# Value products and transposes share two PSUM banks, the MoE output product is turned, and one softmax addition goes to GpSimd

## The chip, the cores and the metric

The kernel runs on one core of one Trainium2 chip. The metric is the device time of one launch in microseconds, as the median of several runs. The profile is that of one more execution, taken by the hardware profiler.

## The reference, cut to what matters

Three stages follow each other: attention that keeps the 32 largest scores of each query, a gated MLP ("MoE 1") and a second MLP with a cosine ("MoE 2"). All arrays are float32.

```python
# q, k, v: (4, 8, 576, 64), batch x heads x sequence x head size
scores = (q @ k.transpose(0, 1, 3, 2)) / sqrt(64)
kth = np.partition(scores, -32, axis=-1)[..., -32:-31]
scores = np.where(scores >= kth, scores, -1e9)
attn = np.exp(scores - scores.max(-1, keepdims=True))
attn = attn / (attn.sum(-1, keepdims=True) + 1e-9)
x = (attn @ v).transpose(0, 2, 1, 3).reshape(2304, 512)

g = x @ w_gate                      # 512 x 1536
x = (g / (1 + exp(-g)) * (x @ w_val)) @ w_out      # 1536 x 512

h = x @ w_in                        # 512 x 2048
out = (h * cos(h)) @ w_out2         # 2048 x 512
```

## The kernel before, in words

**Chunks and units.** The 2304 tokens are cut into ten chunks (`SIZES`, 18 tiles of 128 tokens): two of one tile, "turned" and computed in plain float32, and eight of two tiles, where each operand is split into a high and a low part in a faster float type and each product is three matmuls (high by high, low by high, high by low). A chunk has four head pairs p, and a unit is one tile of one head: 144 units. For a unit, TensorE makes the scores in the two banks `sc` (L572 or L579), ScalarE copies them out (`s`, L584), and VectorE finds the 32 largest by four MAX8 (L609) with three MATCH_REPLACE8 (L612) between. GpSimd makes two bounds of 128x2 and 128x1 (`b`, L623, L627), and ScalarE masks and exponentiates with them (`e`, L640, L651) and sums the row into `sm`.

**From the exponentials to x.** When both heads of a tile are done, TensorE turns `e` in three groups of four, four and one 128x128 transposes into one PSUM bank `tp` (L673), each fetched by ScalarE into `pt` (L679). `tp` is one buffer: a group waits until the one before is fetched (`r_tp = Ring(1)`). When all tiles of a chunk and head pair are in `pt`, `av_proc` multiplies by V into a bank of its own, `av` (L716, L719). Beside it `x_proc` adds 1e-9 to the sums and takes the reciprocal on VectorE, spreads it on GpSimd, turns it in a `tp` buffer, copies it out, and waits for `av` only then:

```python
        yield ("DVE", 0.2, lambda: nc.vector.tensor_scalar(smT[c, p], smT[c, p], 1e-9, None, op0=OP.add), due,
               True)
        yield "DVE", 0.09, rinv, due, True
```

This happens 40 times (ten chunks by four head pairs). ScalarE then copies `av` out (L771), GpSimd multiplies, and the product is split into `XH` and `XL`, which lie in two buffers of a whole chunk each.

**MoE 1.** Per chunk there are twelve steps f. `gemm_proc` makes gate and value for 128 of the 1536 columns (24 matmuls of 256 columns, `gv`, for the last chunk `gvl`, L868). ScalarE and GpSimd make the gated product and split it into `gh` and `gl` (two buffers, `r_g = Ring(2)`), and `wout_proc` (L1146) adds the step to the output product: with the weights `wo` as the held operand and the tokens moving, for each of four 128-column pieces d and three terms one matmul of 256 columns, twelve per step, into two banks `yt`, which hold the transposed result of the chunk:

```python
            def part(d, f=f, k=k):
                w = WO[k]
                gh, gl = G[c, f]
                for i, (a, m) in enumerate(((0, gh), (0, gl), (1, gh))):
                    nc.tensor.matmul(y1p[d // 2][:, d % 2], w[:, a, d * 128:d * 128 + 128], m, ...)
```

After the twelfth step four ScalarE copies through one tile `yo` (L1167), each followed by a store to `y1` in DRAM, free both banks for the next chunk (`r_y1p = Ring(1)`). A copy waits until the store of the one before has landed. For the last chunk but one (`late`) the four copies go to four tiles of their own and wait for no store. The two turned chunks have the tokens held and the weights moving, and turn their result back through `tp` (L1083 to L1123).

**MoE 2.** Six blocks of 384 tokens by sixteen steps: `h` (L1342, 12 matmuls of 384 columns), the cosine on ScalarE and VectorE, and `o` (L1407, 9 matmuls of 512 columns). Its weights `w2` take the place of those of MoE 1 as the steps of the last chunk end (L1270, L1274).

**What sets the order.** Nothing is scheduled at run time. A planner (`class Plan`) runs generators as processes: each step names an engine, a cost, a function that issues the instructions, and a due time. Whenever an engine comes free in the plan, the ready step with the smallest due time is issued, so that each engine gets one fixed queue. `Ring` gives the buffers, `Event` the dependences. On the chip each queue runs in that order and waits on semaphores. All loads and stores named here are issued by SyncE, in its own fixed order. Due times follow `PACE = 4.97` us per unit, and MoE 1 of a chunk is due during the attention of the next.

Of the kernel before, what the change touches and what calls it, by code (L numbers as in the profile page):

```python
# [23 lines left out]
NTOK = B * S  # L24
# [6 lines left out]
CH = 256  # L31
SIZES = (1, 1) + (2,) * 8
# [4 lines left out]
NP = H // 2  # L37
CB = 384
# [120 lines left out]
def topk_attention_moe_moe(ctx: ExitStack, tc: tile.TileContext, qT, kT, vP, w1, wo1, w2, out):  # L159
# [32 lines left out]
    yt = [psL.tile([128, DM], F32, tag=f"y{i}", name=f"y{i}") for i in range(2)]  # L192
    y1p = [x.rearrange("p (a b) -> p a b", a=2) for x in yt]
    sc = psR.tile([128, 2, 512], F32, name="sc")
    av = psR.tile([128, CH], F32, name="av")
# [9 lines left out]
    unit_of = {x: u for u, x in enumerate(units)}  # L205
    NU = len(units)
# [5 lines left out]
    def due_unit(u):  # L212
# [8 lines left out]
            xp.tile([128, 2 * DM], I32, tag="xl", name="c1", bufs=2)[:, :DM]]  # L221
# [46 lines left out]
    def w1_rest(i, raw, due):  # L268
# [4 lines left out]
        r_pre.free(i, t, plan)  # L273
        ev_w1x[f].set(t, plan)
# [110 lines left out]
    kfirst, klast, vfirst = {}, {}, {}  # L385
    for u, (c, p, t, h) in enumerate(units):
        for b, r0, r1 in segments(FIRST[c] + t):
            kfirst.setdefault((c, p, h, b), u)
            klast[c, p, h, b] = u
            vfirst.setdefault((c, p, b), u)  # L390
    vvis = {key: i for i, key in enumerate(vfirst)}
# [12 lines left out]
    ev_q = {(c, p, h): Event() for c in range(NCH) for p in range(NP) for h in range(2)}  # L404
# [10 lines left out]
    def q_due(c, p):  # L415
        return due_unit(unit_of[c, p, 0, 0]) - 25.0

    split = sorted([(k_due(b, p, h), 0, b, p, h) for b, p, h in kb_first] +
                   [(q_due(c, p), 1, c, p) for c in range(RAWC, NCH) for p in range(NP)])
# [5 lines left out]
    def q_index(c, p, h=0):  # L425
        return c * NP + p if c < RAWC else RAWC * NP + ((c - RAWC) * NP + p) * 2 + h

# [37 lines left out]
    def k_proc(i, b, p, h):  # L465
        due = k_due(b, p, h)
        n = NP + kvis[b, p, h]
# [21 lines left out]
    def q_proc(k, c, p):  # L489
        n = SIZES[c] * 128  # L490
        due = q_due(c, p)
# [3 lines left out]
        def load():  # L495
            st["x"] = att.tile([128, 2, HALF], F32, tag="raw", name="qx", bufs=r_kp.n)[:, :, :n]
            for s in range(2):
                nc.sync.dma_start(st["x"][64 * s:64 * s + 64], qT[p, :, FIRST[c] * 128:FIRST[c] * 128 + n]
                                  .rearrange("(h d) n -> d h n", h=2))

        yield "DMA", 1.1, load, due - 10.0, True
        for h in range(2):
            yield r_q.gate(q_index(c, p, h))

            def hi(h=h):
                Q[c, p, h] = att.tile([128, 2, CH], F32R, tag="q", name="q", bufs=r_q.n)[:, :, :n]
                nc.scalar.activation(Q[c, p, h][:, 0], st["x"][:, h], AF.Copy)
# [3 lines left out]
                       lambda h=h: nc.gpsimd.tensor_sub(Q[c, p, h][:, 1], st["x"][:, h], Q[c, p, h][:, 0]),  # L511
                       due + 2.0 * h, True)
            ev_q[c, p, h].set(t, plan)
# [20 lines left out]
    r_s, r_sc, r_w, r_e, r_pt, r_tp, r_av = Ring(5), Ring(1), Ring(2), Ring(2), Ring(1), Ring(1), Ring(1)  # L534
# [3 lines left out]
    eT, smT, ptT, XH, XL = {}, {}, {}, {}, {}  # L538
    ev_x = [Event(NP) for _ in range(NCH)]
    ev_av = {(c, p): Event() for c in range(NCH) for p in range(NP)}  # L540
    ev_pt = {(c, p): Event(SIZES[c]) for c in range(NCH) for p in range(NP)}
    ev_sum = {(c, p): Event(2 * SIZES[c]) for c in range(NCH) for p in range(NP)}
    r_x, r_rs = Ring(2), Ring(1)
    XW = (PLAIN + 1) // 2
    for i in range(XW):
        r_x.freed[i] = Event(min(2, PLAIN - 2 * i))
    xw = {}

    def x_index(c):
        return c // 2 if c < PLAIN else c - PLAIN + XW  # L550

    tp_count = [0]

    def unit_proc(u):
# [3 lines left out]
        st = {}  # L558
        if c < RAWC:
            yield ev_kr[p]  # L560
            yield ev_qr[c, p]
        else:
            for b, r0, r1 in segs:
                yield ev_k[b, p, h]
            yield ev_q[c, p, h]
            q = Q[c, p, h]
        yield r_s.gate(u)

        def qk():
# [5 lines left out]
            for b, r0, r1 in segs[::-1]:  # L575
                k = K[b, p, h]
                for s in range(2):
                    for a in range(2):
                        nc.tensor.matmul(sc[:r1, s, :HALF], q[:, a, t * 128:t * 128 + r1],  # L579
# [8 lines left out]
        if h and (c, t) == (RAWC - 1, SIZES[c] - 1):  # L588
            r_k.free(p, end, plan)
        for b, r0, r1 in segs:  # L590
            if c >= RAWC and kb_last[b, p, h] == u:
                r_k.free(NP + kvis[b, p, h], end, plan)
        if t == SIZES[c] - 1 and (h or c >= RAWC):
            r_q.free(q_index(c, p, h), end, plan)
# [52 lines left out]
        def expo():  # L647
            if (c, p) not in smT:
                smT[c, p] = att.tile([128, 4], F32, tag="sm", name="sm", bufs=3)[:, :2 * SIZES[c]]
            j = 2 * t + h  # L650
            nc.scalar.activation(st["e"], st["e"], AF.Exp, bias=st["b"][:, 2:3], scale=1.0,  # L651
                                 accum_out=smT[c, p][:, j:j + 1])
# [3 lines left out]
        ev_sum[c, p].set(end, plan)  # L656
# [3 lines left out]
    def group_proc(c, p, t, g, made, done):  # L660
# [17 lines left out]
        def fetch():  # L678
            nc.scalar.activation(ptT[c, p][:, j0:j1, t * 128:t * 128 + 128], st["ps"][:, :j1 - j0], AF.Copy)  # L679
# [5 lines left out]
    def pair_proc(c, p, t):  # L685
# [3 lines left out]
        yield r_pt.gate(c * NP + p)  # L689

        def alloc():
            if (c, p) not in ptT:
                ptT[c, p] = att.tile([128, 9, CH], F32, tag="pt", name="pt", bufs=r_pt.n)[:, :, :SIZES[c] * 128]

        now = yield "-", 0.0, alloc, 0.0, True
        made, done = Event(3), Event(3)
        for g in range(3):
            plan.start(group_proc(c, p, t, g, made, done), now)
# [3 lines left out]
        ev_pt[c, p].set(done.time, plan)  # L702

    def av_proc(c, p):
        n = SIZES[c]
        yield ev_pt[c, p]
        segs = segments(FIRST[c], n)
        for b, r0, r1 in segs:
            yield ev_v[c, p, b]
        yield r_av.gate(c * NP + p)  # L710

        def attv():
            pt = ptT.pop((c, p))
# [800 lines left out]
```

## Time and profile before

| | us |
|---|---|
| median of three runs | 1269.52 (1268.78 to 1275.1) |
| the profiled execution, its own time | 1267.64 |
| its span, first to last instruction | 1265.9 |
| attention's last MAX8 ends | some 771 |
| last x of attention | 793.5 |
| MoE 2 alone on TensorE | 868.4 to 1262.3 |

The span is what the trace covers. The time of the profiled execution is 1.7 us longer, and the median of the runs 1.9 us longer again. Times are microseconds from the span's start. TensorE's busy time takes in the pipelined tails of its matmuls, so that the length of a run of matmuls is read from the chain of waits, where their starts are told.

### The profile page before, as it was taken

Reading aid. Unit: us, or ns where it says so; the run is one execution under the profiler, and the core shown is the slowest. Engines: PE = TensorE matmul, PEld = TensorE weight load, DVE = VectorE, ACT = ScalarE, POOL = GpSimd, SP = SyncE. Lnnn points to the kernel's source line nnn. Section 1 sums busy time; section 2 is a strip of 40 time slices with the busy share of each in tenths; the row PEclk is TensorE's granted clock in tenths of the full one; section 3 lists DMA queues with packets and bytes.
Section 4 is the critical chain, followed back from the end, with each engine's and each line's share of the span. In section 5 each row is a group of like instructions: output and inputs, shape, how many; then the busy total and the mean of one; then the engine's idle time right before and its main releaser. Section 6 shows DMA issues by size and latency. Waiting matters only on the chain. (4 is left out here: it accounts for less than half of the span.)

```text
span 1265.9 us, 23359 instructions
## 1 busy us (share of the span) xinstructions
PE 1206.7 (95%) x8040; PEld 1075.1 (85%) x8040; DVE 989.1 (78%) x1978; ACT 916.8 (72%) x2049; POOL 622.8 (49%) x1042
## 2 busy tenths in 40 slices
PE   6699978999999999999999999998999999999998
PEld 3486646998998999889989989997999898999997
DVE  7999999999999999989999993347555555555554
ACT  4689998988998898888887876446555655565554
POOL 4797975776787776777675655543010101010000
PEclk9799989999999999999999999998999999999999
DMA  7645536666566655556553332781010101010000
GB/s 251 200 132 185 172 108 193 206 202 205 170 194 186 192 187 179 179 171 213 188 171 118 114 115 84 250 274 38 1 50 1 51 1 51 1 38 1 12 14 26
DMA packets 84455, 162.20 MB, mean 128 GB/s; under 512 B 17008, under 2 KB 40048, under 8 KB 84336
## 3 DMA queue, kind: packets, MB, share of 16 engines
q1 hardware_dynamic: 84176, 160.65, 39.6%
q8 instruction: 63, 1.03, 0.3%
q14 instruction: 56, 0.46, 0.1%
q10 hardware_dynamic: 160, 0.07, 0.0%
HBM read 133.41 MB, written 27.26 MB: 127 GB/s over the span
## 5 line engine op out<-in xcount | busy, mean ns | idle before, releaser
L609 DVE MAX8 m<-w 128x8 f32<-128x576 f32 x432 | 310.6, 747 | 2.0
L868 PE MATMUL gv<-xh,w 128*128 128x256 f32 x1344 | 289.4, 292 | 2.6 <-ACT hg L836 2.5
L868 PEld LDWEIGHTS gv<-xh,w 128*128 128x128 f32 x1344 | 225.9, 190 | 9.8 <-issue 4.8
L1342 PE MATMUL h<-x2h,w 128*128 128x384 f32 x768 | 214.4, 339 | 1.9 <-DVE g L1376 1.9
L612 DVE MATCH_REPLACE8 w<-m,w 128x576 f32<-128x576 f32 x288 | 212.5, 741 | 0.0
L1407 PE MATMUL o<-w,gh 128*128 128x512 f32 x576 | 196.1, 395 | 0.0
L868 PE MATMUL gv<-xl,w 128*128 128x256 f32 x672 | 189.5, 282 | 0.0
L1146 PE MATMUL y<-gh,wo 128*128 128x256 f32 x768 | 156.8, 287 | 6.3 <-DMA wo<-wo 5.2
L1305 POOL TENSOR_TENSOR x2l<-x,x2h 128x384 fp32r<-128x384 f32 x24 | 25.9, 1078 | 265.7 <-ACT x2h L1294 260.5
L1376 DVE TENSOR_TENSOR g<-r,h 128x384 f32<-128x384 f32 x96 | 53.2, 554 | 121.6 <-ACT r L1371 121.6
L1342 PEld LDWEIGHTS h<-x2h,w 128*128 128x128 f32 x768 | 141.4, 189 | 6.4 <-DVE g L1376 2.3
L1146 PEld LDWEIGHTS y<-gh,wo 128*128 128x128 f32 x768 | 126.5, 192 | 10.6 <-issue 5.9
L1342 PE MATMUL h<-x2l,w 128*128 128x384 f32 x384 | 129.8, 338 | 0.0
L868 PEld LDWEIGHTS gv<-xl,w 128*128 128x128 f32 x672 | 127.9, 190 | 0.2 <-issue 0.2
L673 PE MATMUL tp<-ident,e 128*128 128x128 f32 x648 | 110.7, 281 | 17.5 <-ACT pt L679 15.7
L1369 ACT ACTIVATE r<-r 128x384 f32<-128x384 f32 x96 | 50.3, 524 | 105.3 <-DVE r L1366 105.2
L1407 PEld LDWEIGHTS o<-w,gh 128*128 128x128 f32 x576 | 108.5, 188 | 21.2
L679 ACT ACTIVATE pt<-tp 128x512 f32<-128x512 f32 (+1 forms) x216 | 107.1, 496 | 24.7 <-PE tp L673 23.7
L609 DVE MAX8 m<-s 128x8 f32<-128x576 f32 x144 | 106.0, 744 | 14.5 <-ACT s L584 14.3
L640 ACT ACTIVATE e<-s,b 128x576 f32<-128x576 f32 x144 | 112.7, 783 | 5.1 <-POOL b L623 5.0
L651 ACT ACTIVATE e<-e,b 128x576 f32<-128x576 f32 x144 | 113.1, 785 | 1.9 <-POOL b L627 0.3
L1146 PE MATMUL y<-gl,wo 128*128 128x256 f32 x384 | 111.0, 289 | 2.9 <-DVE gl L930 1.5
(112 smaller groups left out, 2768.8 us busy)
## 6 DMA issues: line engine op xcount, KB each, us to landing
wo<-wo SPq DMA_DIRECT2D x96, 512.0 KB, 3.6
w_raw<-in_w SPq DMA_DIRECT2D x32, 511.8 KB, 4.3
V<-in_vP SPq DMA_DIRECT2D x52, 256.0 KB, 3.0
w<-in_w SPq DMA_DIRECT2D x24, 511.5 KB, 5.5
kx<-in_kT SPq DMA_DIRECT2D x64, 144.0 KB, 3.0
wo<-wo SPq DMA_DIRECT2D x36, 256.0 KB, 3.1
w2d<-w_raw SPq DMA_DIRECT2D x32, 256.0 KB, 2.5
cvx<-w2d SPq DMA_DIRECT2D x32, 256.0 KB, 4.6
```

Source lines behind the costliest of these rows:

```text
L609: nc.vector.max(out=st["m"][:, 8 * i:8 * i + 8], in_=st["w"] if i else st["s"])
L612: nc.vector.match_replace(out=st["w"], in_to_replace=st["m"][:, 8 * i:8 * i + 8], in_values=st["w"] if i else st["s"], imm_value=LOWEST)
L640: nc.scalar.activation(st["e"], st["s"], AF.Prelu, bias=st["b"][:, 1:2], scale=SCALE, alpha=STEEP)
L651: nc.scalar.activation(st["e"], st["e"], AF.Exp, bias=st["b"][:, 2:3], scale=1.0, accum_out=smT[c, p][:, j:j + 1])
L673: nc.tensor.transpose(st["ps"][:, j - j0], e[:, j * 128:j * 128 + 128], ident)
L679: nc.scalar.activation(ptT[c, p][:, j0:j1, t * 128:t * 128 + 128], st["ps"][:, :j1 - j0], AF.Copy)
L868: nc.tensor.matmul(gv[g], W1[f, kk // 2][:, a, g, kk % 2], m[:, kk], start=kk == 0 and i == 0, stop=kk == KT - 1 and i == 2)
L1146: nc.tensor.matmul(y1p[d // 2][:, d % 2], w[:, a, d * 128:d * 128 + 128], m, start=f == 0 and i == 0 and d % 2 == 0, stop=f == NF1 - 1 and ...
L1342: nc.tensor.matmul(st["h"], w[:, a, kk * 128:kk * 128 + 128], m[:, kk], start=kk == 0 and n == 0, stop=kk == KT - 1 and n == 2)
L1369: yield "ACT", 0.41, lambda: nc.scalar.activation(r, r, AF.Abs), due, True
L1376: nc.vector.tensor_mul(st["g"], r, h)
L1407: nc.tensor.matmul(o[t], a[:, cs], W2[f, 1][:, m], start=f == 0 and n == 0, stop=f == NF2 - 1 and n == 2)
```

## The change

- The bank `av` is gone. `tp` has two buffers, and the value product takes one of them; before it does so it waits for the copy of the spread reciprocal (`ev_rs`), because its own copy goes into that reciprocal's tile.
- The addition of 1e-9 goes from VectorE to GpSimd; the reciprocal stays on VectorE.
- In the output product of all chunks the tokens are held and the weights move: for each of the two tiles and three terms one matmul of 512 columns, six per step. The result has tokens on the partitions, so each tile is turned back: per half of a bank a ScalarE copy to `yo`, two transposes into the same half, a second ScalarE copy, and a store. Each bank now has its own ring, one tile each.
- The four tiles of their own for the last chunk but one go; all copies use the one `yo` tile.
- `XH`/`XL` are eight slots, one for each chunk and head pair, freed one by one after the last matmul that reads them. A scratch tile of the weight conversion goes from a slot of x to one of the ten `K` buffers.
- `ATT` would allow attention groups of two tiles and one tile; with the sizes at hand every chunk has one group, as before. Code for a turned last chunk goes; it was not reached.

```diff
-    r_s, r_sc, r_w, r_e, r_pt, r_tp, r_av = Ring(5), Ring(1), Ring(2), Ring(2), Ring(1), Ring(1), Ring(1)
+    r_s, r_sc, r_w, r_e, r_pt, r_tp = Ring(5), Ring(1), Ring(2), Ring(2), Ring(1), Ring(2)
...
+        yield ev_rs[key]
+        k = tp_count[0]
+        tp_count[0] += 1
+        yield r_tp.gate(k)
...
+            av = st["av"] = psR.tile([128, 4, 128], F32, tag="tp", name="av", bufs=r_tp.n).rearrange(
+                "p a b -> p (a b)")[:, :n * 128]
...
+        def fetch():
+            nc.scalar.activation(RX[key], st["av"], AF.Copy)
+
+        end = yield "ACT", 0.07 + 0.1 * n, fetch, due, True
+        r_tp.free(k, end, plan)
+        ev_av[key].set(end, plan)
...
-        yield ("DVE", 0.2, lambda: nc.vector.tensor_scalar(smT[c, p], smT[c, p], 1e-9, None, op0=OP.add), due,
+        yield ("POOL", 0.18, lambda: nc.gpsimd.tensor_scalar(smT[key], smT[key], 1e-9, None, op0=OP.add), due,
                True)
         yield "DVE", 0.09, rinv, due, True
...
+    def wout_proc(c):
+        turned = TURNED[c]
         for f in range(NF1):
             k = c * NF1 + f
             yield ev_g[c, f]
             yield ev_wo[c, f]
+            def part(t, f=f, k=k):
+                bank = yt[(FIRST[c] + t) % NYB]
+                cs = slice(t * 128, t * 128 + 128)
+                g = G[c, f // 2][:, f % 2] if turned else None
+                terms = ((g, WO[k]),) if turned else [(G[c, f][m][:, cs], WO[k][:, a])
+                                                      for m, a in ((0, 0), (1, 0), (0, 1))]
+                for n, (m, w) in enumerate(terms):
+                    nc.tensor.matmul(bank, m, w, start=f == 0 and n == 0, stop=f == NF1 - 1 and n == len(terms) - 1)
+
+            for t in range(SIZES[c]):
+                i = FIRST[c] + t
+                if f == 0:
+                    yield r_y[i % NYB].gate(i // NYB)
+                end = yield "PE", 0.93 if turned else 0.7, lambda t=t, part=part: part(t), moe_due(c, f) + 5.0, False
+                if f == NF1 - 1:
+                    plan.start(y_proc(c, i), end)
...
+    def y_proc(c, i):
+        due = moe_due(c, NF1)
+        bank = yt[i % NYB]
+        y4 = bank.rearrange("p (f n) -> p f n", f=KT)
+        for half in range(2):
+            ko = yo_count[0]
+            yo_count[0] += 1
+            yield r_yo.gate(ko)
+            y2 = y4[:, 2 * half:2 * half + 2]
...
+                nc.scalar.activation(st["y"], y2, AF.Copy)
+            yield "ACT", 0.27, fetch, due, True
...
+                    nc.tensor.transpose(y2[:, j], st["y"][:, j], ident)
+            yield "PE", 0.22, turn, due + 2.0, True
...
+                nc.scalar.activation(st["y"], y2, AF.Copy)
+                nc.sync.dma_start(y1[:, 2 * half:2 * half + 2, i * 128:i * 128 + 128], st["y"])
             end = yield "ACT", 0.27, store, due, True
+            r_yo.free(ko, end + 2.5, plan)
+        r_y[i % NYB].free(i // NYB, end, plan)
```

## Rows read from the trace of the kernel before

**Rows 1.** Busy time by stretch of the end; then clock, DMA share, GB/s.
```profile
770.70:794.00 23.30, 23.30 (x193) 21.00 (x192) 0.35 (x2) 12.75 (x34) 13.28 (x23) 1.00 0.25 78
794.00:808.00 14.00, 11.45 (x95) 11.28 (x94) 4.09 (x7) 5.73 (x15) 7.07 (x7) 0.99 0.82 274
848.00:868.40 20.40, 15.92 (x96) 14.65 (x94) 15.52 (x18) 13.93 (x28) 15.07 (x11) 0.92 0.34 110
868.40:1262.30 393.90, 393.87 (x1959) 355.27 (x1959) 205.61 (x374) 214.93 (x409) 17.25 (x16) 1.00 0.06 19
```
**Rows 2.** The same view by chunk: length, PE, PEld, DVE, ACT, POOL.
```profile
105.00:188.00 83.00, 72.96 (x351) 50.39 (x349) 79.60 (x156) 78.19 (x175) 68.49 (x94) 0.94 0.48 151
270.00:354.00 84.00, 82.58 (x681) 77.03 (x682) 84.00 (x177) 72.61 (x176) 58.71 (x109) 1.00 0.59 186
520.00:604.00 84.00, 81.16 (x674) 76.34 (x675) 78.20 (x157) 70.47 (x168) 61.69 (x107) 1.00 0.60 187
604.00:687.00 83.00, 79.93 (x677) 75.04 (x676) 81.79 (x166) 70.31 (x171) 56.66 (x106) 1.00 0.52 168
```
**Rows 3.** The chain of waits in order of time: start, length, what.
```profile
766.73 1.44 PE y L1146 x12
776.12 0.44 PE tp L673 x4
834.94 2.88 PE gvl L868 x24
868.39 3.48 PE h L1342 x12
874.39 2.08 PE h L1342 x12
876.48 2.09 PE o L1407 x9
```
**Rows 4.** VectorE's queue around one addition: start, length, instruction.
```profile
757.24 0.74 DVE L612 MATCH_REPLACE8 w<-m,w 128x576 f32<-128x576 f32 x1
757.90 0.16 DVE L739 TENSOR_SCALAR sm<-sm 128x4 f32<-128x4 f32 x1
758.02 0.76 DVE L609 MAX8 m<-w 128x8 f32<-128x576 f32 x1
```
**Rows 5.** Groups of instructions by line: busy us, mean ns, idle before.
```profile
L739 DVE TENSOR_SCALAR sm<-sm 128x4 f32<-128x4 f32 (+1 forms) x40 | 13.2, 330 | 7.8 <-ACT e L651 7.8
L627 POOL TENSOR_TENSOR b<-b 128x1 f32<-128x1 f32 x144 | 29.6, 207 | 4.9
L763 ACT ACTIVATE rs<-tp 128x256 f32<-128x256 f32 (+1 forms) x40 | 14.8, 371 | 4.3 <-PE tp L757 4.3
L1407 PEld LDWEIGHTS o<-w,gh 128*128 128x128 f32 x576 | 108.5, 188 | 21.2
```
**Rows 6.** The addition's line and the reciprocal's: ns minimum, median, maximum.
```profile
L739 DVE TENSOR_SCALAR sm<-sm x40: 141/201/1247, 26.9 to 774.8; 128x4 f32<-128x4 f32 x32, 128x2 f32<-128x2 f32 x8
L737 DVE RECIPROCAL sm<-sm x40: 139/155/178, 27.7 to 775.0; 128x4 f32<-128x4 f32 x32, 128x2 f32<-128x2 f32 x8
```
**Rows 7.** Who waited for whom, 200 to 775 or 780: total, times, longest.
```profile
DVE m L609 <- ACT s L584: 6.8, 9, 1.8
DVE sm L739 <- ACT e L651: 5.2, 3, 4.2
PE tp L757 <- ACT pt L679: 2.4, 3, 1.2
PE tp L673 <- ACT pt L679: 2.4, 3, 1.8
```
**Rows 8.** The same over the attention stage, VectorE to 200, GpSimd to 775.
```profile
DVE sm L739 <- ACT e L651: 2.6, 4, 1.0
POOL b L623 <- DVE m L609: 40.1, 38, 3.5
```
**Rows 9.** The copies and stores of y: all, then one chunk; landing in us.
```profile
DMA to landing us min/median/max: 1.7/1.9/5.5
L1167 ACT ACTIVATE yo<-y x4: 378/384/398, 299.7 to 311.0; 128x256 f32<-128x256 f32 x4
```
**Rows 10.** ScalarE's and TensorE's queues around 800: start, length, instruction.
```profile
799.84 1.19 ACT L1167 ACTIVATE yo<-y 128x256 f32<-128x256 f32 x4
806.68 0.36 PE L1146 MATMUL y<-gh,wo 128*128 128x256 f32 x1 [2.55 <-DMA wo<-wo]
```

More of the change, by code (lines that the diff above doesn't have):

```diff
@@ L37 @@
 NP = H // 2
+ATT = [[(0, n)] if n < 3 else [(0, 2), (2, 1)] for n in SIZES]
+NYB = 2
 CB = 384
@@ L273, in w1_rest @@
         r_pre.free(i, t, plan)
+        if i == 2 * NF1 - 1:
+            r_k.free(0, t, plan)
         ev_w1x[f].set(t, plan)
@@ L763, in fetch @@
             nc.scalar.activation(st["x"].rearrange("p (a b) -> p a b", a=n), st["ps"][:, :n], AF.Copy)
[L765 removed]
+        end = yield "ACT", 0.07 + 0.1 * n, fetch, due, True
         r_tp.free(k, end, plan)
[L767 to L774 removed]
+        ev_rs[key].set(end, plan)
@@ L799, in x_proc @@
+            nc.scalar.activation(XH[c, p][:, cols], st["x"], AF.Copy)
+        yield "ACT", 0.07 + 0.1 * n, hi, due, True
+        end = yield ("POOL", 0.05 + 0.0026 * n * 128,
+                     lambda: nc.gpsimd.tensor_sub(XL[c, p][:, cols], st["x"], XH[c, p][:, cols]), due, True)
+        r_rs.free(part_of[key], end, plan)
         ev_x[c].set(end, plan)
@@ L1024, in turned_gemm_proc @@
-        vv = st["vv"]
+        end = yield "ACT", 0.8, evac, due - 10.0, True
+        ring.free(i, end, plan)
+        th, hg, vv = st["th"], st["hg"], st["vv"]
+        yield ("POOL", 0.395,
+               lambda: nc.gpsimd.tensor_scalar(th, th, 1.0, 0.5, op0=OP.add, op1=OP.mult), due, True)
+        yield "POOL", 0.715, lambda: nc.gpsimd.tensor_mul(th, th, hg), due, True
+        end = yield "POOL", 0.715, lambda: nc.gpsimd.tensor_mul(vv, th, vv), due, True
         r_th.free(k, end, plan)
-        stored = not last and fp < NG0
+        stored = fp < NG0
@@ L1078, in turned_wout_proc @@
             yield ev_wo[c, f]
-            def part(f=f, k=k):
-                g = G[c, f // 2]
-                for n, (m, a) in enumerate(((0, 0), (1, 0), (0, 1)) if last else ((0, 0),)):
-                    nc.tensor.matmul(yt[0], g[m][:, f % 2], WO[k][:, a] if last else WO[k], start=f == 0 and n == 0,
-                                     stop=f == NF1 - 1 and (n == 2 or not last))
-            end = yield "PE", 0.7 if last else 0.93, part, moe_due(c, f) + 5.0, False
-            if f % 2 and (last or f // 2 >= NG0):
-                r_g.free(G0[c] + (f // 2 if last else (f // 2 - NG0) // 2), end, plan)
+            def part(t, f=f, k=k):
[13 more added lines that the diff above has]
+                    plan.start(y_proc(c, i), end)
+            if not turned:
+                r_g.free(G0[c] + f, end, plan)
+            elif f % 2 and f // 2 >= NG0:
+                r_g.free(G0[c] + (f // 2 - NG0) // 2, end, plan)
             if c:
@@ L1178, in topk_attention_moe_moe @@
+        r_y[i % NYB].free(i // NYB, end, plan)
+        ev_y1[i].set(end + 2.5, plan)
     O_LAG = 12.0
@@ L1283, in x2_proc @@
         pb = pools["pb"]
-        for c in range(NCH):
-            if FIRST[c] < (j + 1) * TPB and FIRST[c] + SIZES[c] > j * TPB:
-                yield ev_y1[c]
+        for i in range(j * TPB, (j + 1) * TPB):
+            yield ev_y1[i]
         due = b_due(j, 0) - (25.0 if j else 75.0)
@@ L1451, in topk_attention_moe_moe @@
                 plan.start(pair_proc(c, p, t))
-            plan.start(av_proc(c, p))
-            plan.start(x_proc(c, p))
+            for g in range(len(ATT[c])):
+                plan.start(av_proc(c, p, g))
+                plan.start(x_proc(c, p, g))
     for c in range(NCH):
```

442 lines of the change are left out of this document (164 added, 278 removed).

## The prediction

> **What bounds the kernel now.** I read the end first. From 868.4 us TensorE alone sets the time: it is busy for 393.87 of 393.90 us [rows 1], in steps of 2.08 and 2.09 us [rows 3], and the change touches none of them. So everything turns on when this stage starts. Before it, TensorE is without a gap from 770.7 to 794 and idles 2.6 us up to 808 and 4.5 us in 848 to 868.4 [rows 1]. From the last MAX8 at 771 on, the kernel is bound by TensorE's leftover work.
>
> Up to 771 two engines are nearly full. In a chunk of 83 to 84 us VectorE is busy for 78.2 to 84.0, TensorE for 79.9 to 82.6, ScalarE for 70 to 73 [rows 2]. In the early chunks TensorE has more room (72.96 of 83) and VectorE hardly any (79.60) [rows 2]. VectorE has the fixed list of MAX8 and MATCH_REPLACE8, and I take it as the bound up to 771, with TensorE close behind. The sum is therefore VectorE's savings up to 771, then TensorE's additions after it.
>
> **The 1e-9 addition.** It costs 330 ns on average, 13.2 us in all [rows 5]. But the queue is pipelined: in one place the addition starts at 757.90 and the next MAX8 at 758.02 [rows 4], which makes 0.12 us, 40 x 0.12 = 4.8 us. So 4.8 to 13.2 us go; I take the middle, 9.0. The line also waited for ScalarE: 5.2 us after 200, of which 4.2 lie behind the last MAX8, and 2.6 before 200 [rows 7, 8]; 1.0 + 2.6 = 3.6 us go with it.
>
> What is late next is the reciprocal, which stays in VectorE's queue and now waits for GpSimd, with the next unit's MAX8 queued behind it, and ScalarE's masking behind that. GpSimd's smallest operation takes 207 ns [rows 5]; with one such operation ahead of it the addition would end 0.4 us after the exponential. No row shows this wait. Its ends are nothing (the plan puts the reciprocal behind the addition, and GpSimd is so far ahead that it waits 40.1 us for MAX8 results [rows 8]) and 40 x 0.4 = 16 us. I take 0.125 us each, 5 us, nearer to the low end because only seven of forty additions had to wait at all for their exponential (four and three times [rows 7, 8]). Together: -9.0 - 3.6 + 5.0 = -7.6 us, between -16.8 and +11.2.
>
> The skill has a rule that would make more of this. The additions spread from 141 to 1247 ns with a median of 201, the reciprocals on the same data from 139 to 178 [rows 6]. The Trainium skill, "SBUF — State Buffer", "Who interferes with whom", says that VectorE and GpSimd share a pair of ports as an exclusive lock, that a VectorE tensor_scalar can need it, and that the loser is blocked for the whole instruction. The spread agrees with that. By it the full 13.2 us would go and the term would be -13.2 - 3.6 + 5.0 = -11.8 instead of -7.6.
>
> **Two shared banks.** After 200 TensorE waited 2.4 us for a fetch before transposes of `e` and 2.4 us before those of the reciprocal [rows 7]. A second buffer can take away at most these 4.8. They lie beside VectorE's work, and show on the path only as VectorE waits for scores, 6.8 us in the same time [rows 7]. I take -1, between -4.8 and 0.
>
> The value product now waits for the copy of the reciprocal, 0.37 us [rows 5] plus two hand-overs, some 0.8 us as an estimate from it. Behind it in TensorE's queue lie MoE 1 steps that wait with it. In the last pair TensorE had no gap before [rows 1]; up to 0.8 us, I take +0.5.
>
> **The turned output product.** A step was 12 matmuls in 1.44 us. Nine matmuls of 512 columns take 2.09 us, so six take 1.39 [rows 3]. That is 0.05 us per step, 4.5 us over 8 x 12 = 96 steps. New are four transposes per tile, 16 x 4 = 64, at 0.44 / 4 = 0.11 us [rows 3]: 7.0 us. TensorE gets 2.5 us more work, 0.3 per chunk, and its idle time of 1.4 to 3.1 us per chunk up to 771 covers that [rows 2]. After 771 come 17 steps (204 matmuls of y start there), and the transposes of the last two chunks, 16: -0.8 + 1.8 = +1.0 us, on the path. If the cover before 771 is gone, it is 2.5 in place of 1.0.
>
> ScalarE gets 32 copies more at 0.384 us [rows 9], 12.3 us, 1.5 per chunk. It has 9 to 13 us per chunk free [rows 2], so I cost them at nothing; without that cover 1.5 us per chunk would stand before the score copies for which VectorE waits.
>
> **Draining the banks.** In the middle chunks the four copies of y already span 11 us (299.7 to 311.0 [rows 9]) because each waits for the store before it, and TensorE has attention to do meanwhile. At the last boundary this is different. The last chunk but one drained in one burst of 1.19 us at 799.84, without waiting for stores, and the next y matmul came at 806.68 after 2.55 us of idle TensorE, for its weights [rows 10]. Now four halves take turns on one tile. Each costs two copies (0.77), two transposes (0.22) and a store of 1.9 to 5.5 us [rows 3, 9], 2.9 to 6.5 us. The second bank is free after three halves and one more pair of copies with its transposes: 9.7 to 20.5 us after 799.84, at 809.5 to 820.3. That is 2.8 to 13.6 us later than 806.68. Until then TensorE has MoE 1 steps of 2.88 us [rows 3], but only until their buffers are full: two of `gh`/`gl`, two before them, three banks, some five steps or 14.4 us from 794, to 808 without what is left of chunk eight. The plan knows the drain (with 2.5 us a store) and will put this work ahead. I take +2, between 0 and +13.6.
>
> **Other edits.** The finer slots of x, the moved scratch tile and the deleted code add no instruction. Slots come free earlier, a wait that no row shows; 0. SyncE issues as many stores as before.
>
> **The sum.** -7.6 - 1 + 0.5 + 1.0 + 2 = -5.1 us. Against the profiled execution's own 1267.64 this is 1262.5; the median of the runs lies 1.9 us higher, so 1264.4 us. A measurement of this kernel tells 0.5%, 6.3 us, from no change: faster is below 1263.2, slower above 1275.9.
>
> **Rivals.**
> - *VectorE sets the pace alone and the whole addition goes.* For it: the additions' long records [rows 6], and VectorE at 84.0 of 84 us [rows 2]. Against: the 0.12 us between two starts [rows 4], and TensorE with 1.4 us to spare in that chunk. -16.8 + 5 for the addition, nothing for the drain, +1.0 - 1 + 0.5: -11.3, 1258.2 us. Chance 0.20.
> - *TensorE is the bound already.* VectorE's savings turn into waits for scores. For it: TensorE at 82.58 of 84 [rows 2], with 6.8 us of such waits there now [rows 7]. Against: VectorE is as full or fuller in three of the four chunks shown. Then only additions are left, 2.5 + 2 + 0.5 = +5.0: 1274.5 us. Chance 0.16.
> - *The last drain costs its whole price*, the slower side. Place: the boundary between the last two chunks, where stores compete with weight loads at a DMA share of 0.82 [rows 1]. A `yo` copy that waits for a store also holds up the tanh and the weight conversions behind it in ScalarE's queue. It decides once it outweighs the rest, -7.1 us, that is when y starts later than 816.5 by this reckoning; at 820.3 it is +13.6, the sum +6.5: 1276 us, and with the addition worth only half, 1280. For it: 5.5 us is a landing of this very store. Against: the median is 1.9. Chance 0.17.
> - *Fewer weight loads speed the product up.* The rows say no: 512 columns with a load of 188 ns [rows 5] take 232 ns each, the time of two of 256. The Trainium skill, "TensorE: Matmul & The Clock Gate", "Back-to-back issue gap", says that the spacing is set by load and matmul together and gives 131 ns per matmul at 512 columns. By it six take 0.79 us, and the 17 steps after 771 would save 11 us: 1253 us. Chance 0.01.
> - *The change does nothing that counts*, both full engines keeping their lengths: 1269 us. Chance 0.02.
>
> **How the numbers follow.** The forecast has 0.44, from 1259 to 1269. Faster: 0.4 of the forecast's share, the first rival and the fourth, 0.18 + 0.20 + 0.01 = 0.39. Slower: three quarters of the drain's share and a little of the second rival, 0.13 + 0.03 = 0.16. The rest, 0.45, is within 0.5%. The range from 1253 to 1278 leaves out the far end of each rival, about 2 in 10.
>
> **What would show it.** Right: the last MAX8 ends at 762 to 766; the reciprocals have waits for GpSimd of some 5 us in total; six y matmuls take 1.39 us; ScalarE is 12 us busier; MoE 2 runs alone from about 863. Wrong: more waits of MAX8 for scores, with the last MAX8 still at 770 (second rival); a gap of TensorE at the last boundary of several us, ended by a y copy or its store (third); the waits of the reciprocal above 10 us, in which case the addition was cheaper where it was.

## The result and the profile after

The changed kernel takes 1255.64 us (median of 4, 1253.74 to 1256.97), the kernel before 1269.15 in the same comparison: a ratio of 0.9894 [0.9871, 0.9917], 13.5 us less. The forecast was 1264.4, in a range of 1253 to 1278; the first rival had 1258.2. The profiled execution took 1255.94 us, its span 1253.9 against 1265.9.

Where did the 12.0 us of span go? The first view is busy time by stretch of the end of the kernel after, as in [rows 1] (PE, PEld, DVE, ACT, POOL, then clock, DMA share, GB/s):

```profile
763.00:785.50 22.50, 22.50 (x164) 19.12 (x163) 0.18 (x1) 12.06 (x32) 12.64 (x22) 1.00 0.26 87
785.50:800.00 14.50, 14.50 (x118) 14.24 (x117) 7.91 (x12) 9.04 (x22) 11.06 (x11) 1.00 0.84 281
840.00:862.70 22.70, 19.76 (x111) 17.26 (x110) 19.55 (x25) 17.85 (x38) 14.13 (x10) 1.00 0.28 90
862.70:1250.00 387.30, 387.30 (x1937) 349.51 (x1936) 201.72 (x367) 212.60 (x403) 17.35 (x16) 1.00 0.06 20
```

From 862.7 us TensorE runs on without a gap, where the kernel before did from 868.4, and more of MoE 2 is done by then: 64 matmuls of `h` and 18 of `o`, against 48 and 9. The last MAX8 ends at 762.97, in the kernel before at 770.66. So 7.7 us came before the last MAX8, and 12.0 - 7.7 = 4.3 us after it: from there to the end of the span it is 490.9 us instead of 495.2.

*Before the last MAX8.* The next lines are the stretch up to the last MAX8, before and then after, each from its own trace:

```profile
0.00:770.66 770.66, 722.19 (x5393) 633.20 (x5394) 744.94 (x1546) 649.19 (x1524) 551.10 (x971) 0.98 0.55 175
```
```profile
0.00:762.97 762.97, 718.58 (x4965) 609.54 (x4966) 730.36 (x1507) 653.12 (x1549) 560.73 (x1011) 0.99 0.56 177
```

VectorE is busy for 744.94 and 730.36 us, 14.6 less; its idle time rises from 25.7 to 32.6. The groups of the kernel after say part of why (busy us, mean ns, idle before), beside [rows 5]:

```profile
L770 DVE RECIPROCAL sm<-sm 128x4 f32<-128x4 f32 (+1 forms) x40 | 6.7, 168 | 13.6 <-POOL sm L772 13.4
L772 POOL TENSOR_SCALAR sm<-sm 128x4 f32<-128x4 f32 (+1 forms) x40 | 9.6, 240 | 6.5 <-ACT e L665 3.7
L1107 ACT ACTIVATE yo<-y 128x256 f32<-128x256 f32 x36 | 14.8, 412 | 2.4 <-PE y L1102 2.3
L1096 ACT ACTIVATE yo<-y 128x256 f32<-128x256 f32 x36 | 14.5, 402 | 3.9 <-DMA y<-yo 3.1 <-PE y L1063 0.7
```

The addition's 13.2 us are gone from VectorE and stand on GpSimd as 9.6. The reciprocal, which waited for nothing before, now waits 13.4 us for GpSimd. The list of waits of VectorE shows how much of it lies before the last MAX8 (up to 200 us, then 200 to 770; total, times, longest):

```profile
DVE sm L770 <- POOL sm L772: 3.5, 6, 1.2
...
DVE sm L770 <- POOL sm L772: 9.9, 9, 6.2
DVE m L623 <- ACT s L598: 5.8, 11, 1.6
```

6.2 of the 9.9 lie behind the last MAX8, so 7.2 us stand before it, against 3.6 for the addition before [rows 7, 8]. On TensorE the waits for fetches of the transposes of `e`, 15.7 us up to the last MAX8 in the kernel before, are 3.3:

```profile
PE tp L673 <- ACT pt L679: 15.7, 18, 2.4
```
```profile
PE tp L790 <- POOL rx L779: 6.9, 3, 3.1
PE tp L687 <- ACT pt L693: 3.3, 6, 0.9
```

A new wait stands beside them, the first of these two lines: 6.9 us in which transposes of the reciprocal wait for GpSimd's spread, all before 53 us (0.4 in the kernel before). In the first 270 us both kernels run 192 MAX8, so these two profiles show no gain from the early part of the stage.

*After it.* The output product is as counted: the chain of waits has six matmuls of 512 columns in 1.39 us, where [rows 3] had twelve of 256 in 1.44. Behind them on the chain stand a store of y and a load of `wo`, then the steps of MoE 2:

```profile
791.11 1.39 PE y L1063 x6
...
797.02 3.51 DMA y<-yo
...
807.12 5.75 DMA wo<-wo
...
870.78 2.12 PE h L1279 x12
872.90 2.09 PE o L1344 x9
```

### The profile page after: what moved, and what is told of

Read it like the earlier page. It is cut to its first block, busy times and chain, and to the rows that moved or that the text cites. A ratio compares the mean times of both kernels' runs of the same rounds, so it can differ in the third digit from the quotient of the medians.

```text
span 1253.9 us, 22487 instructions
## 1 busy us (share of the span) xinstructions
PE 1200.3 (96%) x7528; PEld 1043.6 (83%) x7528; DVE 975.1 (78%) x1938; ACT 923.8 (74%) x2081; POOL 632.0 (50%) x1082
## 4 chain that ended last, share of the span: by engine, by line
PE 58%; DMA 8%; ACT 6%; POOL 3%; DVE 2%; issue 2%; SPq 0%; POOLq 0%; ACTq 0%
PE o L1344 16%; PE h L1279 15%; PE gv L899 10%; PE y L1063 7%; PE av L743 2%; PE sc L593 2%; DMA wo<-wo 2%; DMA kx<-in_kT 2%; PE tp L687 2%; PE gvl L899 2%; DMA y<-yo 1%; DMA w_raw<-in_w 1%; DMA qx<-in_qT 1%; ACT e L654 1%; POOL K L496 1%
## 5 line engine op out<-in xcount | busy, mean ns | idle before, releaser
L899 PE MATMUL gv<-x,w 128*128 128x256 f32 x2016 | 283.7, 288 | 1.7 <-ACT hg L866 1.6
L899 PEld LDWEIGHTS gv<-x,w 128*128 128x128 f32 x2016 | 259.0, 190 | 8.6 <-ACT hg L866 2.8
L1063 PE MATMUL y<-wo,gh 128*128 128x512 f32 x400 | 148.5, 413 | 6.7 <-DMA wo<-wo 5.1
L1344 PE MATMUL o<-w,gl 128*128 128x512 f32 x288 | 113.6, 394 | 1.0 <-DVE gl L1327 1.0
L598 ACT ACTIVATE s<-sc 128x576 f32<-128x576 f32 x144 | 95.4, 662 | 21.6 <-PE sc L586 16.2
L626 DVE MATCH_REPLACE8 w<-m,s 128x576 f32<-128x576 f32 x144 | 106.9, 742 | 0.0
L693 ACT ACTIVATE pt<-tp 128x512 f32<-128x512 f32 (+1 forms) x216 | 101.9, 503 | 4.9 <-PE tp L687 3.3
L687 PE MATMUL tp<-ident,e 128*128 128x128 f32 x648 | 99.4, 277 | 5.9 <-ACT pt L693 3.3
L1327 DVE TENSOR_TENSOR gl<-g,gh 128x384 fp32r<-128x384 f32 x96 | 56.4, 588 | 58.0 <-ACT gh L1324 58.0
```

The lines of the kernel that those rows point to most:

```text
L598: nc.scalar.activation(st["s"], sc[:, :, :HALF], AF.Copy)
L626: nc.vector.match_replace(out=st["w"], in_to_replace=st["m"][:, 8 * i:8 * i + 8], in_values=st["w"] if i else st["s"], imm_value=LOWEST)
L687: nc.tensor.transpose(st["ps"][:, j - j0], e[:, j * 128:j * 128 + 128], ident)
L693: nc.scalar.activation(pt[:, j0:j1], st["ps"][:, :j1 - j0], AF.Copy)
L899: nc.tensor.matmul(gv[g], W1[f, kk // 2][:, a, g, kk % 2], m, start=kk == 0 and i == 0, stop=kk == KT - 1 and i == 2)
L1063: nc.tensor.matmul(bank, m, w, start=f == 0 and n == 0, stop=f == NF1 - 1 and n == len(terms) - 1)
```

## The experiments

The theories, by the letters of the expectations: A, the addition's place makes the gain; B, the banks make it; C, the turned product does; later D, the parts pay only together, each alone is given back; and E, the order of the queues alone makes the differences.

The twelve were measured in three groups, each on one chip beside the kernel before. The kernel before has another median in each (1266.6 us on one chip, 1271.6 and 1267.0 on a second), so I compare ratios. 0.01 is 12.7 us. The table gives for each profile the end of the last MAX8, from there to the end of the span, and how many MAX8 run between 270 and 520 us (those that cross an end are counted), where the two-tile chunks run evenly.

| kernel | addition on | `tp` buffers | y product | last MAX8 | to the end | MAX8, 270 to 520 | ratio [95%] |
|---|---|---|---|---|---|---|---|
| before | VectorE | 1 + `av` | weights held | 770.7 | 495.2 | 196 | 1 |
| b_jitter, other order | VectorE | 1 + `av` | weights held | 774.7 | 491.4 | 197 | 0.9988 [0.9969, 1.0007] |
| j_before, second order | VectorE | 1 + `av` | weights held | 780.0 | 491.8 | 193 | 1.0048 [1.0028, 1.0067] |
| b_add_pool | GpSimd | 1 + `av` | weights held | 771.9 | 491.2 | 194 | 0.9997 [0.9980, 1.0014] |
| j_b_add_pool, second order | GpSimd | 1 + `av` | weights held | 773.6 | 492.3 | 194 | 0.9981 [0.9961, 1.0001] |
| a_tp1 | GpSimd | 1 shared | turned | 775.7 | 492.9 | 193 | 1.0029 [1.0014, 1.0045] |
| a_banks_only | VectorE | 2 shared | weights held | 777.3 | 493.8 | 194 | 0.9993 [0.9968, 1.0018] |
| a_add_dve | VectorE | 2 shared | turned | 768.9 | 491.0 | 198 | 0.9980 [0.9962, 0.9998] |
| j_a_add_dve, second order | VectorE | 2 shared | turned | 762.8 | 490.7 | 199 | 0.9916 [0.9895, 0.9938] |
| a_y_straight | GpSimd | 2 shared | weights held | 764.3 | 493.7 | 198 | 0.9925 [0.9902, 0.9948] |
| after | GpSimd | 2 shared | turned | 763.0 | 490.9 | 200 | 0.9894 [0.9871, 0.9917] |
| j_after, second order | GpSimd | 2 shared | turned | 760.1 | 491.1 | 201 | 0.9881 [0.9858, 0.9903] |
| a_yo_late | GpSimd | 2 shared | turned | 765.0 | 489.6 | 199 | 0.9882 [0.9850, 0.9915] |
| a_no_add | left out | 2 shared | turned | 765.4 | 495.8 | 197 | 0.9942 [0.9922, 0.9962] |

**The addition alone (b_add_pool).**

```diff
-        yield ("DVE", 0.2, lambda: nc.vector.tensor_scalar(smT[c, p], smT[c, p], 1e-9, None, op0=OP.add), due,
+        yield ("POOL", 0.18, lambda: nc.gpsimd.tensor_scalar(smT[c, p], smT[c, p], 1e-9, None, op0=OP.add), due,
```

> The kernel before, with the addition of 1e-9 alone moved to GpSimd. Theory A (the addition leaving VectorE's queue shortens the attention stage, and the rest came at the end): the last MAX8 ends some 8 us earlier than in the kernel before, at 763 us, and the time falls to 1261 to 1262 us. Theory B (the second transpose buffer and the shared bank made the gain): 1269 us, last MAX8 still at 771. Theory C (the turned output product made it): 1269 us as well. By either theory the reciprocals wait 7 to 13 us for GpSimd.

It gave nothing: 0.9997, last MAX8 at 771.88. VectorE's busy time fell, but only by 7.3 us to 737.60, and its idle time rose by 8.6 to 34.3. The line is the stretch up to the last MAX8, and below it are the waits of VectorE and TensorE in it, after one line of the kernel before:

```profile
0.00:771.88 771.88, 718.66 (x5393) 632.04 (x5394) 737.60 (x1507) 649.67 (x1524) 560.01 (x1010) 0.98 0.54 175
```
```profile
DVE m L609 <- ACT s L584: 14.3, 12, 6.6
```
```profile
DVE m L609 <- ACT s L584: 19.2, 13, 6.7
DVE sm L737 <- POOL sm L739: 3.9, 6, 1.3
...
PE tp L673 <- ACT pt L679: 18.3, 24, 2.6
```

The waits for scores grew from 14.3 us to 19.2, and TensorE's waits for transposes from 15.7 to 18.3. Theory A falls for this order. That the longer waits for scores come from the saving is not shown: b_jitter, further down, has 19.4 us of them with nothing saved.

**The addition put back (a_add_dve).**

```diff
-        yield ("POOL", 0.18, lambda: nc.gpsimd.tensor_scalar(smT[key], smT[key], 1e-9, None, op0=OP.add), due,
+        yield ("DVE", 0.2, lambda: nc.vector.tensor_scalar(smT[key], smT[key], 1e-9, None, op0=OP.add), due,
```

> The changed kernel, with the addition of 1e-9 alone put back on VectorE. Theory A: the last MAX8 moves back to 770 to 772 us and the time rises by 8 us to 1263 to 1264 us. Theories B and C: it stays at 1255 to 1257 us.

0.9980: in the new kernel the addition's place is worth 0.9980 - 0.9894 = 0.0086, 10.9 us. VectorE's busy time is 9.5 us higher than after:

```profile
0.00:768.94 768.94, 719.61 (x4967) 613.14 (x4968) 739.84 (x1546) 653.31 (x1549) 550.51 (x972) 0.98 0.54 175
```

Theory A asked for 8 us more and a last MAX8 at 770 to 772 us; it has the direction and about the size, and B and C do not.

**One transpose buffer (a_tp1).**

```diff
-    r_s, r_sc, r_w, r_e, r_pt, r_tp = Ring(5), Ring(1), Ring(2), Ring(2), Ring(1), Ring(2)
+    r_s, r_sc, r_w, r_e, r_pt, r_tp = Ring(5), Ring(1), Ring(2), Ring(2), Ring(1), Ring(1)
```

> The changed kernel with one transpose buffer in place of two; value products and transposes then share one bank. Theory A: VectorE is still the bound, at most 3 us more, 1256 to 1259 us. Theory B: TensorE again waits some 10 us or more for the fetches of the transposes, and the value product adds its own waits; 1263 us or more, with the last MAX8 later by what is lost.

1.0029, 17 us more than the changed kernel and slower than the kernel before. The last MAX8 ends 12.7 us later. VectorE idles 40.1 us up to it, the most of all runs, and TensorE's waits for transposes are back, with those of the value product for the reciprocal's copy beside them:

```profile
0.00:775.67 775.67, 723.51 (x4960) 609.57 (x4961) 735.54 (x1507) 655.42 (x1546) 557.66 (x1009) 0.98 0.54 174
```
```profile
PE tp L687 <- ACT pt L693: 14.8, 19, 2.0
PE av L740 <- ACT rs L796: 6.1, 7, 1.8
```

This is theory B's number. It has the value product in the same single bank as well, which the kernel before had not, so it is not the buffer by itself.

**The output product as before (a_y_straight).**

```diff
-        plan.start(wout_proc(c))
+        plan.start((wout_proc if TURNED[c] else straight_wout_proc)(c))
```

`straight_wout_proc` is the `wout_proc` of the kernel before, on the new rings.

> The changed kernel with the output product of the two-tile chunks as before: weights held, twelve matmuls of 256 columns per step, four copies per chunk, four tiles of their own for the last chunk but one. Theory A: the last MAX8 stays at 762 to 764 us, and what changes is the end: TensorE loses 64 transposes and gains 4.5 us of matmuls, 1254 to 1258 us. Theory C: the 4 us that came at the end (from the last MAX8 to the last instruction) are lost again, 1260 us, with the lower granted clock back at the last boundary.

0.9925 against 0.9894. The intervals overlap, so the turned product is worth between nothing and some 8 us, 3.9 by the medians. The last MAX8 is 1.3 us later, the end 2.8 us longer. The granted clock at the last boundary, which theory C wanted lower, did not fall. The time alone does not decide between A and C.

**The banks without the other two (a_banks_only).** The two diffs above, together.

> The changed kernel with both the addition back on VectorE and the output product as before (weights held), so that the shared banks and the slots of x are what is left of the change. Theory D (two engines are full at once, VectorE by its list and TensorE by its waits for the single transpose buffer, and each part alone is given back by the other engine): 1263 to 1267 us, with TensorE's waits for fetches of the transposes below 6 us but the last MAX8 not before 768. Theory B (the banks alone made the gain): 1257 us or less.

0.9993, last MAX8 at 777.3. As theory D had it, the banks alone give nothing in this order, though the ratio stands for 1268 us, above its 1263 to 1267. With the addition on GpSimd the same banks give 0.9997 - 0.9925 = 0.0072, 9 us (b_add_pool and a_y_straight). TensorE's waits for `e`'s transposes came to 8.2 us, not to below 6:

```profile
PE tp L790 <- POOL rx L779: 14.6, 5, 4.1
PE tp L687 <- ACT pt L693: 8.2, 10, 2.7
```

**No addition at all (a_no_add).** The addition is left out of the computation.

```diff
-        yield ("POOL", 0.18, lambda: nc.gpsimd.tensor_scalar(smT[key], smT[key], 1e-9, None, op0=OP.add), due,
-               True)
```

> The changed kernel without the addition of 1e-9 (left out altogether; each sum holds an exponential of 0 and is at least 1). The reciprocal then waits for ScalarE directly. If VectorE's 7.2 us of waits for GpSimd before the last MAX8 are on the path: 4 to 7 us less than the changed kernel, 1249 to 1252 us. If TensorE is again the bound once the addition is gone: no change, 1255 us.

Neither: 0.9942 is 6 us slower than the changed kernel, with less to do. Of the 7.3 us between the two profiles, 2.5 lie before the last MAX8 and 4.8 after. The waits of the reciprocal fell from 7.2 to 4.8 us, so the 7.2 us of waits were not what could still be gained. I had no theory for the loss, and it made me doubt differences of this size.

**Tiles of their own at the last boundary (a_yo_late).**

```diff
...
+            late = c == NCH - 2
+            if late:
+                yield ev_pb
+            else:
+                yield r_yo.gate(ko)
...
+                if late:
+                    st["y"] = pools["pb"].tile([128, 2, 128], F32, tag=f"yo{i % 2}{half}", name="yo")
...
```

> The changed kernel with four tiles of their own for the copies of y of the last chunk but one, as the kernel before had. By the prediction's term for the drain (2 us, at most 13.6) the last boundary gets shorter: 1252 to 1254 us. If the MoE 1 steps put ahead cover the drain: no change, 1255 to 1256 us.

0.9882 against 0.9894: no difference that can be measured, give or take some 5 us. The first y matmul of the last chunk now starts 3.8 us after the first copy (797.73 after 793.95) instead of 10.2 (802.04 after 791.85), and the time stays, so most of the drain is covered by other work. The 2 us that the prediction gave it cannot be told from nothing.

**The same instructions in another order (b_jitter).**

```diff
-        yield ("DVE", 0.2, lambda: nc.vector.tensor_scalar(smT[c, p], smT[c, p], 1e-9, None, op0=OP.add), due,
+        yield ("DVE", 0.33, lambda: nc.vector.tensor_scalar(smT[c, p], smT[c, p], 1e-9, None, op0=OP.add), due,
```

> The kernel before with the same instructions; only the planner's cost for the addition is 0.33 in place of 0.2 us, so that the fixed order of the queues comes out otherwise. It measures what a change of order by itself does. Theory D needs it to be small: within 3 us of the kernel before, 1264 to 1270 us. If it moves the time by 6 us or more, differences of that size between the other kernels can be order alone.

The time stayed (0.9988), but its parts did not: the last MAX8 came 4.0 us later and the rest was 3.8 us shorter. One profile's split into stages is therefore good to about 4 us. Up to the last MAX8, VectorE's busy time is 4.3 us lower than in the kernel before, and its waits for scores are 19.4 us:

```profile
0.00:774.71 774.71, 726.39 (x5395) 636.57 (x5396) 740.62 (x1546) 648.59 (x1524) 549.30 (x971) 0.97 0.56 174
```
```profile
DVE m L609 <- ACT s L584: 19.4, 10, 6.7
```

**A second order for four kernels.** The planner's cost of the reciprocal is changed in all four in the same way; no instruction changes.

```diff
-        yield "DVE", 0.09, rinv, due, True
+        yield "DVE", 0.16, rinv, due, True
```

> The changed kernel under a second order of the queues: same instructions, the planner's cost of the reciprocal 0.16 in place of 0.09 us. Theory D (the addition must leave VectorE and TensorE must lose its waits for the single transpose buffer; only both together shorten the attention stage): a ratio of 0.985 to 0.993 to the kernel before, last MAX8 at 761 to 766 us. Rival E (the gain is a lucky order of the queues): 0.995 or more.

> The kernel before with the addition alone moved to GpSimd, under the same second order (reciprocal planned at 0.16 us). Theory D: no gain again, a ratio of 0.996 to 1.003, last MAX8 at 769 us or later. Rival E: anything, down to 0.99.

> The changed kernel with the addition back on VectorE, under the same second order. Theory D: little gain, a ratio of 0.995 to 1.002, last MAX8 at 768 us or later. Rival E: anything, down to 0.99.

> The kernel before under the same second order. Theory D: a ratio of 0.997 to 1.003, last MAX8 at 769 to 777 us. Rival E: anything from 0.99 to 1.005.

| | order 1 | order 2 |
|---|---|---|
| before | 1 | 1.0048 |
| addition moved | 0.9997 | 0.9981 |
| banks and product changed | 0.9980 | 0.9916 |
| both | 0.9894 | 0.9881 |

The whole change holds under both orders: the ratios of the kernel before in three orders (1, 0.9988, 1.0048) and of the changed kernel in two (0.9894, 0.9881) lie apart. j_after was as theory D expected (its last MAX8 came 0.9 us before 761), j_b_add_pool too, j_before came out a little above its range, and j_a_add_dve fell out of it: 0.9916 with the last MAX8 at 762.8, where D asked for 768 or later. So theory D does not hold in general. Rival E does not explain the whole change, but it explains much of the difference between its parts: the order moved j_a_add_dve by 0.0064 and j_before by 0.0048, 8 and 6 us. The granted clock is a rival that the runs do not separate: its mean is 0.984 to 0.985 over the runs of the kernel before and 0.994 over those of the changed one. It does not make the gain alone: a_add_dve and j_after both have 0.991, and their ratios are 0.0099 apart.

In order 1 the parts give 0.4 and 2.5 us alone and 13.5 together; in order 2, counted from j_before, 8.5, 16.8 and 21.2. The average over orders and over the other part's state is the firmest statement these runs allow, and a rough one: the move of the addition is worth (0.0003 + 0.0067 + 0.0086 + 0.0035) / 4 = 0.0048, 6 us (0.4 to 10.9 singly), and the banks with the product (0.0020 + 0.0132 + 0.0103 + 0.0100) / 4 = 0.0089, 11 us (2.5 to 16.8 singly). With such a scatter of four, the first is not clear of nothing.

The busy time of VectorE up to the last MAX8 goes the same way in all four comparisons. It is not free of the order, though: the same instructions take 744.94, 740.62 and 749.63 us in the kernel before, b_jitter and j_before. The lines are j_before, j_b_add_pool, j_a_add_dve and j_after:

```profile
0.00:780.03 780.03, 722.44 (x5397) 632.43 (x5397) 749.63 (x1546) 649.55 (x1525) 549.99 (x971) 0.98 0.53 173
```
```profile
0.00:773.55 773.55, 723.82 (x5395) 635.45 (x5396) 737.45 (x1507) 648.28 (x1524) 558.06 (x1010) 0.98 0.53 175
```
```profile
0.00:762.81 762.81, 715.18 (x4970) 607.40 (x4971) 741.30 (x1546) 653.78 (x1551) 551.16 (x972) 0.99 0.55 177
```
```profile
0.00:760.13 760.13, 713.10 (x4967) 610.32 (x4968) 731.24 (x1507) 652.44 (x1550) 561.30 (x1011) 0.98 0.56 177
```

The move lowers it by 12.2 and 10.1 here, by 7.3 and 9.5 in order 1. The idle time takes 3.5 to 8.6 us of it back. The banks and the product lower busy time by 5.1 to 8.3 us in all four comparisons. Idle time falls from 30.4 to 21.5 and from 36.1 to 28.9 here; in order 1 it falls by 1.7 in one comparison and rises by 3.4 in the other.

## Why the prediction was right, and where it was not

*Right in its range, partly by luck.* The measured time lies in the range because the range was wide: the terms gave -5.1 us and the change gave -13.5. VectorE stayed the fullest engine up to the last MAX8 (730.4 of 763.0 us) with TensorE close behind (718.6), as forecast; but b_add_pool shortened VectorE's list by 7.3 us and gained nothing, so VectorE is not the bound by itself. MoE 2 alone keeps its steps of 2.08 to 2.12 and 2.09 us. Of the marks that the prediction named, these came in: last MAX8 at 763.0 (762 to 766 forecast), six y matmuls in 1.39 us, waits of the reciprocal of 7.2 us (5). TensorE's last gap ends at 862.7 (863), but with more of MoE 2 done than the kernel before had at 868.4, so that mark agrees by luck. ScalarE is busy for 923.8 us over the span instead of 916.8, 7 us more and not 12.

*The addition.* The term was -7.6 us; its average over four comparisons is -6, between -0.4 and -10.9. Its saving was put at 9.0 us of VectorE's time, a middle chosen between 4.8 and 13.2 without a row, and busy time fell by 7.3 to 12.2. The trace of the kernel before has the number: from the start of each addition to the start of VectorE's next instruction, the 40 take 10.3 us in all. The 0.12 us of [rows 4] was one of the cheap ones. The wait for GpSimd was rightly put at the low end of its bounds. The upper bound of +11.2 leaves the -3.6 out; with it the term ends at +7.6. All 20 additions of more than 200 ns end 22 to 30 ns after a GpSimd instruction that had started before them and from which they read nothing; the other 20 take 141 to 189. In a_add_dve all 23 such additions end 21 to 30 ns after one. The trace agrees with the rule that the prediction cites, the Trainium skill, "SBUF — State Buffer", "Who interferes with whom", that the loser is blocked. The 10.3 us are less than the full 13.2 because VectorE's next instruction starts before the record of the addition ends. In the longest case the next MAX8 starts 1.17 us after the addition:

```profile
613.46 1.32 POOL L240 TENSOR_TENSOR w_raw<-c,w_raw 128x512 int32<-128x512 int32 x1 [0.47 <-ACT w_raw L238]
```
```profile
613.56 1.25 DVE L739 TENSOR_SCALAR sm<-sm 128x4 f32<-128x4 f32 x1
614.73 0.75 DVE L609 MAX8 m<-w 128x8 f32<-128x576 f32 x1
```

Put back on VectorE in the new kernel the addition took 377 ns on average, on GpSimd 240; VectorE's reciprocal takes 139 to 178 in the kernel before [rows 6].

*The two shared banks: the term that was mis-sized.* I bounded it by the 4.8 us that TensorE waits for fetches after 200 us, and took -1, because VectorE bounds the stage. The banks with the product are worth some -11 us on average, and with one shared buffer, which also holds the value product, 17 us more are needed. What failed is the bound: a wait of TensorE was priced at its own length. The waits before 200 us, 13.3 us of the 15.7, were left out without a reason, but the profiles before and after do not show that they count: both run 192 MAX8 in the first 270 us. The counts of MAX8 between 270 and 520 us say more. Kernels that differ in the banks and the product alone have 196 and 198, 194 and 200, 193 and 199, 194 and 201: 2 to 7 MAX8 more, at 250 / 200 = 1.25 us some 2.5 to 9 us, while TensorE waits in that stretch for only 2.8 to 3.8 us for fetches in the kernels with one buffer. (The counts depend on the stretch; from 300 to 550 us the kernels with one buffer and with two overlap. From 240 to 760 us 393 to 399 MAX8 start with one buffer, 399 to 405 with two and 395 in a_banks_only.) So the cost reaches further than the waits that are listed. How, these runs show only in part; the last section has a count that bears on it.

*The turned product.* The sums per step are right (1.39 against 1.44 us). ScalarE's copies of y take 29.3 us where they took 12.3 and the turned chunks' 3.2, and a_y_straight, without most of them, is no faster, so this stayed hidden, as forecast, though [rows 2] leave ScalarE 11.4 to 13.5 us per chunk, and 4.8 in the first one shown, and not 9 to 13. Whether the product gains anything is within the intervals. The rule on spacing, the Trainium skill, "TensorE: Matmul & The Clock Gate", "Back-to-back issue gap", does not hold here: 232 ns per matmul, not 131.

*The end.* The terms after the last MAX8 were +1.0, +0.5 and +2, and the two profiles differ by -4.3. The prediction misread the place in the kernel before: 806.68 is the second step of the last chunk, whose first y matmul came at 800.74, 0.9 us after the first copy. Its threshold of 816.5 is a slip as well; by its own terms it is 806.68 + 7.1 = 813.8. The drain was the feared one in form: the copies of y came one by one (first copies at 791.85, 795.49, 800.61 and 804.64), and the next y matmul came at 802.04, 10.2 us after the first copy. But the planned MoE 1 steps filled the time, and TensorE's one long gap there was again for weights, 1.69 us where it was 2.55 [rows 10]:

```profile
813.01 0.47 PE L1063 MATMUL y<-wo,gh 128*128 128x512 f32 x1 [1.69 <-DMA wo<-wo]
```

Most of the 4.3 us are not the change's. Of the kernels with the old banks and product, the other four profiles need 491.2 to 492.3 us from the last MAX8 to the end, where the kernel before needed 495.2 and the four with the new banks and product in the two orders need 490.7 to 491.1. Its last MAX8, at 770.7, is also the earliest of the five with the old ones (771.9 to 780.0), so this one pair of profiles seems to put too little of the gain before the last MAX8. The +3.5 us of the terms were too much: beside this profile, the comparisons of the banks and the product give -0.3 to -1.2 there. The granted clock of the kernel before fell there: 0.96 over 100 us, at most 4 us by estimate. The first fence is the kernel before, 100 us from the last MAX8 and three stretches of 5 us in it, the second the kernel after:

```profile
770.66:870.66 100.00, 92.87 (x699) 88.92 (x698) 40.45 (x63) 54.32 (x122) 54.48 (x55) 0.96 0.57 190
805.00:810.00 5.00, 3.32 (x20) 3.35 (x21) 0.42 (x1) 1.43 (x3) 1.01 (x1) 0.78 0.94 311
860.00:865.00 5.00, 5.00 (x26) 4.86 (x26) 5.00 (x5) 3.36 (x8) 5.00 (x4) 0.75 0.08 26
870.00:875.00 5.00, 5.00 (x20) 4.50 (x20) 2.83 (x6) 2.95 (x7) 0.00 (x0) 0.73 0.16 43
```
```profile
762.97:862.97 100.00, 94.41 (x631) 84.79 (x630) 43.24 (x65) 57.56 (x131) 53.97 (x55) 1.00 0.58 190
```

*The rivals.* The first, with VectorE alone as the pace, named about the nearest time for a reason that only holds in part: the addition's 10.3 us, but not VectorE alone. The fourth, at 1253 us, is as near, and is refuted by the 1.39 us of six matmuls. The second, TensorE as the bound already, was refuted as a whole. b_add_pool looks like its mechanism, VectorE's savings turning into waits for scores, but b_jitter has as much of these waits without a saving. The third, the drain at its whole price, is refuted by the time itself and by a_yo_late.

## What to carry to other kernels

When two engines are both nearly full, a saving on one can fail to show because the other or the order of the queues takes it back, so test parts together and not only one by one. A short wait of an engine that feeds the bound is not priced by its length: try the second buffer. Read the price of a small VectorE instruction from its start to the next start, and look at what GpSimd runs beside it. And where a planner fixes the order of the queues, run each comparison under a second order of the same instructions before a difference of half a per cent is put down to a cause.

## What was not expected of the hardware

VectorE's busy time for the same MAX8 and MATCH_REPLACE8 is not constant. With two units in hand a round for both (two MATCH_REPLACE8 and two MAX8) takes 750.39 - 747.50 = 2.9 us, 1.45 per unit; with one unit in hand, the dependent pair takes 760.56 - 758.91 = 1.65 us. The lines are VectorE's queue in the kernel after:

```profile
747.50 0.07 DVE L626 MATCH_VALUE_LOAD w<-m,w 128x8 f32 x1
...
748.95 1.41 DVE L623 MAX8 m<-w 128x8 f32<-128x576 f32 x2
750.39 0.09 DVE L626 MATCH_VALUE_LOAD w<-m,w 128x8 f32 x1
...
758.91 0.76 DVE L623 MAX8 m<-w 128x8 f32<-128x576 f32 x1
...
760.56 0.76 DVE L623 MAX8 m<-w 128x8 f32<-128x576 f32 x1
```

From a MAX8 to the next match, or back, it is 0.66 us start to start where the units alternate, and 0.78 to 0.80 where one unit follows itself, as between the last two lines. Up to the last MAX8 the slow kind occurs 129 times in the kernel before and 102 times after, 93 in b_jitter, 164 in j_before and 159 in b_add_pool; 93 to 164 times with one buffer and 82 to 123 with two. At 0.12 to 0.14 us each, the 30 more in b_add_pool take 3.7 of the 10.3 us of the addition back, which leaves about the 7.3 us that were seen. The 27 fewer after the whole change give 3.3 us, with the 10.3 most of the 14.6 by which VectorE's busy time fell. So a score that comes late may cost more than the wait that is listed, because the unit before runs alone meanwhile. That fits part of the price of the banks; that late scores are the cause is not shown.

The granted clock was 1.00 (2.4 GHz) through the last boundary in the kernel after, in spite of gaps of TensorE of 1.69 and 1.48 us. In the kernel before it fell three times, to 0.73 to 0.78 in 5 us stretches, a mix of 2.4 and 1.2 GHz: after a gap of 2.55 us, at two gaps of 1.07 and 1.54 us close together, and after one of 1.86 us.
